# Other PSUM banks for two small pieces of a fused block: the first w1 group and the first segment's attention

## The chip, the cores and the metric

The kernel runs on one core of one Trainium2 chip. The time of a run is the device time in microseconds. Before the change six runs gave a median of 1535.79 us (1535.21 to 1541.54). One further execution was recorded by the hardware profiler; all rows shown here come from it, and their times are microseconds from the start of its span.

## What is computed

Cut to what matters (all inputs bf16):

```python
xn = layernorm(A_x)                                  # 2048 tokens of 1024
return A_x + _A_ref(xn, ...) + _B_ref(xn, ...)

def _A_ref(x, mem0, Wq, Wk, Wv, Wo, seg_len):        # 32 heads of 128, 8 memory rows, segments of 32
    mem = mem0
    for s in range(64):
        h = concat([mem, x[32 * s : 32 * s + 32]])   # 40 rows
        q, k, v = h @ Wq, h @ Wk, h @ Wv
        o = softmax(mask(q @ k.T * scale)) @ v @ Wo  # memory rows see all, tokens causally
        mem = o[:8]
        outs.append(o[8:])

def _B_ref(x, w1, w2, w3, w4):
    h = gelu(layernorm(x) @ w1)
    x1 = x + shifted(h) @ w2                         # four quarters of the columns, shifted by -1, +1, -2, +2 tokens
    return x1 + gelu(layernorm(x1) @ w3) @ w4
```

## The kernel before

TensorE (PE in the profile) does all products, into PSUM, which the kernel divides by hand: a ring of four banks, one bank a tile (`mm_tile`, lines 132 to 133), and two groups of two banks each, "A" and "B", one tile at a time in each (`aux_tile`, line 135). A new tile in "A" or "B" must wait until everything that reads the old one is done. Every engine works in the order in which the program issues its instructions: the order is written out by hand, and no scheduler changes it.

The work goes in four stages.

*Stage 1, the product with w1 (lines 170 to 313).* Tokens are in 16 tiles of 128 rows. For each tile VectorE (DVE) takes mean and variance (`ln_stats`, L202 to L206; the power on GpSimd, POOL, L207), and `ln_apply` (L218) writes the normalised rows. These are transposed to xn2T: for tiles 0 to 3 on PE (`pe_trans`, L247), with the first half of the columns copied out by DVE (L250) and the second by ScalarE (ACT, L252); from tile 4 on by a transposing DMA (`dma_trans`, L223). Two tiles make a group g of 256 tokens. For each group there are eight column tiles `co` of 128 outputs, each a chain of eight matmuls of 256 columns over the contraction (L262) and then a gelu on ACT (L264). Between column tiles 3 and 4 of a group, ACT normalises tiles of x in place (`normalise_x`, L235): four of them in group 1, two in later groups. After each group `seg_sums` (L257) forms two small products, in "A" and "B". `warm(n)` issues n matmuls of 512 columns on a constant (L197).

Group 0 is written apart (L270 to L296). Its first six column tiles do the first four contraction steps, as soon as half of w1 is there. They are held in the four ring banks and in group "A", one bank each. Then tiles 2 and 3 are normalised and transposed, both through group "B", then come the second halves, and then column tiles 6 and 7 whole.

*Stages 2 and 3* are the product with w2 and the second layernorm (L329 to L343), and the products with w3 and w4 (L502, L520). They are not touched, but at the end of stage 3 the buffers of the attention are set up (`att_prep`).

*The attention.* Blocks b of 512 tokens, eight steps hg in each, four heads in a step; a step makes Q (L567), K (L583) and V (L590) in twelve chains c = 0 to 11. Between chains stand hooks for the step before (p) and the one before that (pp): `scores(p, m)` for m = 0 to 3 at c = 0, 3, 6, 9, into "A" (L612), read by the exponentials on ACT (L616); and `values` into "B" (L642), read by an addition on DVE (L646) and then a small copy on ACT (L650). `values(pp, 3)` stands at c = 1, and `values(p, 0)`, `(p, 1)`, `(p, 2)` at c = 4, 7, 10. Between the exponentials and L646 stand, on DVE, the softmax of the scores (L618 to L631), whose result `BD` the values of that m use one or more chains later.

In block 0 the first segment has the given memory mem0, and so each of its eight steps also does a small ordinary attention over 40 rows, in the following step (i = 1 to 8), through three hooks:

- `first_soft` at c = 2: psVZ (L666, four products that turn the memory's values), copied out by ACT (L667), and psZ (L671, the scores), read by DVE (L673), then a softmax on DVE and ACT (L675 to L681)
- `first_trans` at c = 6: psZT (L687), copied out by ACT (L689)
- `first_values` at c = 8: psZO (L695), read by DVE (L696) and ACT (L697)

All four take a bank of the ring. Their operands have 8 or 40 rows or columns, so the weight loads have shapes 128x8, 128x40, 40x40 and 40x128. `first_scores` (L654 to L661) copies the operands together on POOL. In steps 5 to 7 DVE also prepares the next block's input, `make_xm` (L469), at c = 2, 6 and 10.

*The end.* `out_part` multiplies the attention's output with Wo, 32 matmuls of 512 columns for a tile (L740), DVE adds what the other branch left (L746) and a DMA stores the tile (L748). The last tile is `out_chain(b, 7)` (L900).

Of the kernel before, what the change touches and what calls it, by code (L numbers as in the profile page):

```python
# [21 lines left out]
P = 128  # L22
# [41 lines left out]
def kernel(  # L64
# [98 lines left out]
    with ExitStack() as keepx:  # L163
# [6 lines left out]
        with ExitStack() as p0:  # L170
# [65 lines left out]

            def pe_trans(n):
                xn2 = xn2s.pop(n)
                if n < 2:
                    ps = [mm_tile("psT")[:], mm_tile("psT")[:]]  # L240
                else:
                    t = aux_tile([P, 2, 512], "B", "psT")
                    ps = [t[:, 0, :], t[:, 1, :]]
                for h in range(2):
                    p3_ = ps[h].rearrange("p (k t) -> p k t", k=4)
                    for k in range(4):
                        nc.tensor.matmul(p3_[:, k, :], xn2[:, (4 * h + k) * P:(4 * h + k + 1) * P], ident[:], start=True, stop=True)  # L247
                    dst = xn2Ts[n // 2][:, n % 2, 4 * h:4 * h + 4, :]
                    if h == 0:
                        nc.vector.tensor_copy(dst, p3_)  # L250
                    else:
                        nc.scalar.copy(dst, p3_)  # L252
# [22 lines left out]
            warm(2)  # L275
            ln_apply(1)
            pe_trans(1)
            warm(2)
            normalise_x(0)
            normalise_x(1)  # L280
            first = [mm_tile("ps1")[:, 0:256] for _ in range(4)]
            t = aux_tile([P, 2, 512], "A", "ps1")
            first += [t[:, 0, 0:256], t[:, 1, 0:256]]
            for co in range(6):
                w1_part(0, co, first[co], range(4))
            ln_stats(2)
            ln_stats(3)
            for n in (2, 3):
                ln_apply(n)
            for n in (2, 3):  # L290
                pe_trans(n)
            for co in range(6):
                w1_part(0, co, first[co], range(4, KT))
            stage1(0, (6, 7))
            seg_sums(0)
            seg_sums(1)  # L296
            ln_stats(4)
# [54 lines left out]
    with ExitStack() as p3:  # L352
# [130 lines left out]
        def att_prep():  # L483
            load_xT(0)
            for nm in "qkv":
                need_w(nm, 0)
            need_w("q", 1)
            make_xm(0)
            sm = A["sm"]
            A["BD"] = [sm.tile([P, 4, TW], BF16, name=f"BD{i}") for i in range(3)]  # L490
            A["EQ"] = [sm.tile([P, 4, W], F32, name=f"EQ{i}") for i in range(2)]
            for t in A["EQ"]:
                nc.gpsimd.memset(t[:, :, SEG:W], float(M))
            A["SS"] = sm.tile([P, 4], F32, name="SSsum")
            nc.gpsimd.memset(A["SS"][:], 0.0)

# [43 lines left out]
    def hsl(hg):  # L540
        return slice(4 * hg, 4 * hg + 4)
# [96 lines left out]
    def values(s, m):  # L638
# [10 lines left out]
            VM[:, hsl(s.hg), z + j0:z + 4].unsqueeze(3).to_broadcast((P, 4, 4 - j0, SEG)), op=ALU.add)  # L649
        nc.scalar.copy(oTm[:, hsl(s.hg), z:z + 4], p4[:, :, :, SEG])  # L650

    def first_scores(s):
        QZ = smp.tile([P, 4, L], BF16, tag="QZ", name="QZ")
        KZ = smp.tile([P, 4, L], BF16, tag="KZ", name="KZ")  # L654
        nc.gpsimd.tensor_copy(QZ[:, :, 0:SEG], s.Q[:, :, 0:SEG])
        nc.gpsimd.tensor_copy(QZ[:, :, SEG:L], QM[:, hsl(s.hg), 0:M])
        nc.gpsimd.tensor_copy(KZ[:, :, 0:SEG], s.K[:, :, 0:SEG])
        nc.gpsimd.tensor_copy(KZ[:, :, SEG:L], s.K[:, :, 512:512 + M])
        s.VZ = smp.tile([L, 512], BF16, tag="VZ", name="VZ")
        nc.gpsimd.tensor_copy(s.VZ[0:SEG, :], s.V[0:SEG, 0, :])  # L660
        s.QZ, s.KZ = QZ, KZ  # L661

    def first_soft(s):
        pv = mm_tile("psVZ")
        for hh in range(4):
            nc.tensor.matmul(pv[SEG:L, hh * P:(hh + 1) * P], VM[:, 4 * s.hg + hh, 0:M], ident[:], start=True, stop=True)  # L666
        nc.scalar.copy(s.VZ[SEG:L, :], pv[SEG:L, :])  # L667
        ps = mm_tile("psZ")
        p3_ = ps[0:L, 0:4 * L].rearrange("p (h k) -> p h k", h=4)
        for hh in range(4):  # L670
            nc.tensor.matmul(p3_[:, hh, :], s.QZ[:, hh, :], s.KZ[:, hh, :], start=True, stop=True)  # L671
        e = smp.tile([L, 4, L], F32, tag="eZ", name="eZ")
        nc.vector.scalar_tensor_tensor(e[:], p3_, SCALE, mask40[0:L, :].unsqueeze(1).to_broadcast((L, 4, L)), op0=ALU.mult, op1=ALU.add)  # L673
        mx = smp.tile([L, 4], F32, tag="mxZ", name="mxZ")
        nc.vector.tensor_reduce(mx[:], e[:], axis=AX.X, op=ALU.max)  # L675
        nc.vector.tensor_tensor(e[:], e[:], mx[:].unsqueeze(2).to_broadcast((L, 4, L)), op=ALU.subtract)
        nc.scalar.activation(e[:], e[:], ACTF.Exp)
        nc.vector.tensor_reduce(mx[:], e[:], axis=AX.X, op=ALU.add)
        nc.vector.reciprocal(mx[:], mx[:])
        s.PZ = smp.tile([L, 4, L], BF16, tag="PZ", name="PZ")  # L680
        nc.vector.tensor_tensor(s.PZ[:], e[:], mx[:].unsqueeze(2).to_broadcast((L, 4, L)), op=ALU.mult)  # L681

    def first_trans(s):
        ps = mm_tile("psZT")
        p3_ = ps[0:L, 0:4 * L].rearrange("p (h k) -> p h k", h=4)
        for hh in range(4):
            nc.tensor.matmul(p3_[:, hh, :], s.PZ[:, hh, :], ident[0:L, 0:L], start=True, stop=True)  # L687
        s.PZT = smp.tile([L, 4, L], BF16, tag="PZT", name="PZT")
        nc.scalar.copy(s.PZT[:], p3_)  # L689

    def first_values(s):
        ps = mm_tile("psZO")
        p3_ = ps[:, 0:4 * L].rearrange("p (h k) -> p h k", h=4)
        for hh in range(4):
            nc.tensor.matmul(p3_[:, hh, :], s.VZ[:, hh * P:(hh + 1) * P], s.PZT[:, hh, :], start=True, stop=True)  # L695
        nc.vector.tensor_copy(oX[:, hsl(s.hg), 0:SEG], p3_[:, :, 0:SEG])  # L696
        nc.scalar.copy(oZ[:, hsl(s.hg), :], p3_[:, :, SEG:L])  # L697

    rms = {}

# [30 lines left out]

    parts = {}

    def out_part(b, c, h0, h1):
        m, ch = divmod(c, 2)
        if h0 == 0:
            parts[b, c] = mm_tile("psP")
        ps = parts[b, c]
        for h in range(h0, h1):
            nc.tensor.matmul(ps[:], oX[:, h, m * P:(m + 1) * P], wo_sb[:, h, ch * 512:(ch + 1) * 512], start=(h == 0), stop=(h == H - 1))  # L740
        if h1 < H:
            return
        cc = slice(ch * 512, (ch + 1) * 512)
        Rt = Rts.pop((b, c))
        ot = iop.tile([P, 512], BF16, tag="ot", bufs=2, name="ot")
        nc.vector.tensor_tensor(ot[:], ps[:], Rt[:], op=ALU.add)  # L746
        eng = nc.sync if b == NB - 1 else nc.gpsimd
        eng.dma_start(out_v[:, 4 * b + m, cc], ot[:])  # L748
        if c + 2 < 8:
            load_Rt(b, c + 2)  # L750

    def out_chain(b, c):
# [50 lines left out]
    for i in range(NS):  # L803
# [7 lines left out]
        def at(c, f, *a):  # L811
            hooks.setdefault(c, []).append((f, a))
# [10 lines left out]
                at(2 + 4 * (k % 3), make_xm, s.b + 1, (k,))  # L823
        if fz:
            at(2, first_soft, p)
            at(6, first_trans, p)
            at(8, first_values, p)
            first_scores(p)
        if s.hg == 1 and s.b > 0:
# [38 lines left out]
        if last:  # L868
            b = s.b
            load_Rt(b, 0)  # L870
            load_Rt(b, 1)
            hp = H - 4
            scores(s, 0)
            values(p, 3)
            out_part(b, 0, 0, hp)
            scores(s, 1)
            values(s, 0)
            out_part(b, 1, 0, hp)
            scores(s, 2)
            values(s, 1)  # L880
            out_part(b, 0, hp, H)
            out_part(b, 1, hp, H)
            out_part(b, 2, 0, hp)
            scores(s, 3)
            values(s, 2)
            out_part(b, 3, 0, hp)
            values(s, 3)
            out_part(b, 2, hp, H)
            out_part(b, 3, hp, H)
            norm_sums(b)  # L890
            for j in range(4):
                norm_recip(b, j)
            norm_apply(b)
            norm_add(b)
            out_chain(b, 4)
            out_chain(b, 5)
            verify()
            out_chain(b, 6)
            verdict()
            out_chain(b, 7)  # L900

    main.close()
    cond = nc.values_load(flag_i[0:1, 0:1], min_val=0, max_val=NV + 1)
# [126 lines left out]
```

## Time and profile before

| what | value |
|---|---|
| median of six runs | 1535.79 us |
| time of the profiled execution | 1534.74 us |
| its span | 1533.0 us |
| PE busy | 1506.6 us, 98% of the span |
| VectorE (DVE) busy | 662.5 us, 43% |
| ScalarE (ACT) busy | 450.4 us, 29% |
| GpSimd (POOL) busy | 232.0 us, 15% |
| granted PE clock over the span | 0.998 |
| one step of block 0 in the attention (psS of step 2 to psS of step 3) | 26.7 us |

How to read the rows: a row of the time-ordered view gives the start, the duration, the engine, the line of the kernel, the operation, what is written from what, the shape and how many instructions were merged; in brackets, for how long the engine was idle before it and which instruction's end released it. A merged row of several matmuls lasts until the last of them has ended, and the next one can start before that, since matmuls are pipelined. "PEld" rows are the weight loads ahead of the matmuls. The table by stretches gives for each stretch its length, the busy time of each engine with the number of instructions in parentheses, the granted PE clock (1.00 is full speed), the busy share of the DMA engines and GB/s.

### The profile page before, as it was taken

Reading aid. Unit: us, or ns where it says so; the run is one execution under the profiler, and the core shown is the slowest. Engines: PE = TensorE matmul, PEld = TensorE weight load, DVE = VectorE, ACT = ScalarE, POOL = GpSimd, SP = SyncE. Lnnn points to the kernel's source line nnn. Section 1 sums busy time; section 2 is a strip of 40 time slices with the busy share of each in tenths; the row PEclk is TensorE's granted clock in tenths of the full one; section 3 lists DMA queues with packets and bytes.
Section 4 is the critical chain, followed back from the end, with each engine's and each line's share of the span. In section 5 each row is a group of like instructions: output and inputs, shape, how many; then the busy total and the mean of one; then the engine's idle time right before and its main releaser. Section 6 shows DMA issues by size and latency. Waiting matters only on the chain.

```text
span 1533.0 us, 23861 instructions
## 1 busy us (share of the span) xinstructions
PE 1506.6 (98%) x9425; PEld 792.3 (52%) x9552; DVE 662.5 (43%) x1562; ACT 450.4 (29%) x1241; POOL 232.0 (15%) x640
## 2 busy tenths in 40 slices
PE   7999999999999999999999999999999999999998
PEld 5944444444444466666544544444544444444445
DVE  7275010010110225666632767731667641676652
ACT  4633202103012034444410443320443420334320
POOL 3133020111110111212110111110111110111100
PEclk9999999999999999999999999999999999999999
DMA  6679653454121545474422454431454441344211
GB/s 185 168 217 304 225 178 105 149 179 153 62 90 42 191 140 177 139 203 155 152 86 66 138 165 138 152 103 49 137 162 143 139 131 55 115 142 142 88 36 36
DMA packets 190885, 208.38 MB, mean 136 GB/s; under 512 B 51176, under 2 KB 158712, under 8 KB 190768
## 3 DMA queue, kind: packets, MB, share of 16 engines
q1 hardware_dynamic: 183520, 182.49, 39.6%
q0 software_dynamic: 7248, 24.31, 4.1%
q8 instruction: 77, 1.26, 0.4%
q14 instruction: 40, 0.33, 0.1%
HBM read 170.07 MB, written 25.17 MB: 127 GB/s over the span
## 4 chain that ended last, share of the span: by engine, by line
PE 92%; DVE 5%; ACT 1%; DMA 1%; issue 1%; SPq 0%; POOL 0%; ACTq 0%; DVEq 0%
PE psP L740 14%; PE psV L590 14%; PE psK L583 13%; PE ps L502 13%; PE ps L520 13%; PE psQ L567 12%; PE ps L329 4%; PE ps L262 3%; PE psO L642 2%; PE psS L612 2%; PE psM L599 1%; DMA x<-in_A_x_dram 1%; ACT ET L616 1%; DVE Q L574 1%; DVE BD L631 1%
## 5 line engine op out<-in xcount | busy, mean ns | idle before, releaser
L740 PE MATMUL psP<-wo_sb,oX 128*128 128x512 bf16 x1003 | 221.4, 379 | 1.1
L616 ACT ACTIVATE ET<-psS 32x132 f32<-32x132 f32 x512 | 139.0, 272 | 196.3 <-PE psS L612 191.1
L520 PE MATMUL ps<-w,hT_all 128*128 128x512 bf16 x874 | 193.7, 379 | 1.2
L583 PE MATMUL psK<-xT,w 128*128 128x512 bf16 x747 | 176.4, 379 | 1.1
L567 PE MATMUL psQ<-xT,w 128*128 128x512 bf16 x750 | 175.9, 379 | 1.5 <-DVE Q L574 0.4
L590 PE MATMUL psV<-w,xT 128*128 128x512 bf16 x745 | 175.1, 379 | 1.0
L583 PEld LDWEIGHTS <-w 128*128 128x128 bf16 x1280 | 121.4, 98 | 81.2 <-issue 0.8
L740 PEld LDWEIGHTS <-oX 128*128 128x128 bf16 x1024 | 99.7, 98 | 118.4
L567 PEld LDWEIGHTS <-w 128*128 128x128 bf16 x1024 | 97.0, 98 | 105.6 <-issue 2.9
L503 ACT ACTIVATE hT_all<-ps 128x512 bf16<-128x512 f32 x112 | 66.7, 597 | 283.9 <-PE ps L502 283.9
L520 PEld LDWEIGHTS <-hT_all 128*128 128x128 bf16 x896 | 87.0, 98 | 103.9
L650 ACT CAST oTm<-psO 128x16 bf16<-128x16 f32 x128 | 23.0, 179 | 355.9 <-DVE oX L646 355.9
L618 DVE STREAM_TRANSPOSE EQ<-ET 128x128 f32<-128x128 f32 x128 | 39.7, 310 | 184.0 <-ACT ET L616 184.0
L574 DVE TENSOR_TENSOR Q<-psQ,QM 128x512 bf16<-128x512 f32 (+1 forms) x128 | 85.6, 678 | 61.6 <-ACT Q L573 42.3
L633 POOL TENSOR_TENSOR BD<-ET,c_segone_sb 128x16 bf16<-128x16 f32 x128 | 33.9, 265 | 517.3 <-ACT ET L616 517.3
L590 PEld LDWEIGHTS <-xT 128*128 128x128 bf16 x768 | 72.1, 98 | 73.5
L502 PE MATMUL ps<-xn3T,w3a 128*128 128x512 bf16 x448 | 97.7, 379 | 0.0
L502 PE MATMUL ps<-xn3T,w3b 128*128 128x512 bf16 x448 | 97.7, 379 | 0.0
L631 DVE TENSOR_TENSOR BD<-PT,c_segone_sb 128x512 bf16<-128x512 bf16 x128 | 89.9, 702 | 4.4
L746 DVE TENSOR_TENSOR ot<-psP,Rt 128x512 bf16<-128x512 f32 x32 | 22.0, 691 | 156.2 <-PE psP L740 156.2
L646 DVE TENSOR_TENSOR oX<-psO,VM 128x512 bf16<-128x512 f32 (+1 forms) x128 | 86.3, 674 | 2.0 <-PE psO L642 2.0
L433 DVE TENSOR_SCALAR xt<-xt,lnst 128x1024 bf16<-128x1024 bf16 x16 | 8.7, 546 | 181.1 <-POOL R L432 181.1
(149 smaller groups left out, 1608.9 us busy)
## 6 DMA issues: line engine op xcount, KB each, us to landing
w<-in_A_Wq_dram SPq DMA_DIRECT2D x32, 1024.0 KB, 5.7
w<-in_A_Wk_dram SPq DMA_DIRECT2D x32, 1024.0 KB, 5.8
w<-in_A_Wv_dram SPq DMA_DIRECT2D x32, 1024.0 KB, 5.7
R_scratch<-x POOLq DMA_DIRECT2D x16, 512.0 KB, 6.0
R<-R_scratch SPq DMA_DIRECT2D x16, 512.0 KB, 7.7
chunk<-in_A_Wv_dram SPq DMA_DIRECT2D x8, 1024.0 KB, 6.4
R_scratch<-R POOLq DMA_DIRECT2D x16, 512.0 KB, 6.6
chunk<-in_A_Wo_dram SPq DMA_DIRECT2D x8, 1024.0 KB, 6.4
```

Source lines behind the costliest of these rows:

```text
L329: nc.tensor.matmul(ps[:], hTB[:, k, o:o + P], w2_sb[:, k, ch * 512:(ch + 1) * 512], start=(k == 0), stop=(k == KT - 1))
L502: nc.tensor.matmul(ps[:], w3[:, k, (f % FH) * P:(f % FH + 1) * P], xn3Ts[tb][:, :, k, :], start=(k == 0), stop=(k == KT - 1))
L503: nc.scalar.activation(h3T[:, f, :], ps[:], ACTF.Gelu_apprx_tanh)
L520: nc.tensor.matmul(ps[:], h3T[:, f, j * P:(j + 1) * P], w4t[f // 4][:, f % 4, ch * 512:(ch + 1) * 512], start=(f == 0), stop=(f == FT - 1))
L567: nc.tensor.matmul(ps[:], w[:, k, hh * P:(hh + 1) * P], s.xm[:, k, 0:512], start=(k == 0), stop=(k == KT - 1))
L574: nc.vector.tensor_tensor(q3[:, j0:16, 0:SEG], p3_[:, j0:16, :], QM[:, 4 * s.hg + hh, z + j0:z + 16].unsqueeze(2).to_broadcast((P, 16 - j0 ...
L583: nc.tensor.matmul(ps[:, 0:c], w[:, k, hh * P:(hh + 1) * P], s.xm[:, k, h2 * c:(h2 + 1) * c], start=(k == 0), stop=(k == KT - 1))
L590: nc.tensor.matmul(ps[:], s.xm[:, k, m * P:(m + 1) * P], w[:, k, :], start=(k == 0), stop=(k == KT - 1))
L616: nc.scalar.activation(ET[q, :, :], ps[q, :, W * j:W * (j + 1)], ACTF.Exp, scale=SCALE)
L631: nc.vector.tensor_tensor(B4[:, :, :, 0:SEG], PT[:].unsqueeze(2).to_broadcast((P, 4, 4, SEG)), so.unsqueeze(3).to_broadcast((P, 4, 4, SEG) ...
L646: nc.vector.tensor_tensor(oX[:, hsl(s.hg), m * P:(m + 1) * P].rearrange("p h (j i) -> p h j i", i=SEG)[:, :, j0:4, :], p4[:, :, j0:4, 0:SE ...
L740: nc.tensor.matmul(ps[:], oX[:, h, m * P:(m + 1) * P], wo_sb[:, h, ch * 512:(ch + 1) * 512], start=(h == 0), stop=(h == H - 1))
```

## The change

There are three edits.

1. **Group 0 of stage 1.** All eight column tiles do their first four contraction steps at once. They lie two to a bank in the four banks of "A" and "B"; only the first of a bank starts the accumulation with the start flag. The second halves follow in pairs, each pair with its two gelus, and the transposes of tiles 2 and 3, now always in ring banks, stand after the second and third pair. The `warm(2)` ahead of the group is gone.
2. **The small attention.** The operands QZ, PZ, VZ and a new one, VMZ, are 128 rows or columns wide, with zeros beyond the 40 or 8 that count; they are allocated once and cleared on POOL in `att_prep`. One more POOL copy a step fills VMZ. Their products go to "A" (psZ, psZT) and "B" (psVZ, psZO) instead of the ring. `first_trans` moves from c = 6 to c = 5.
3. **The last output tile** is done in two halves of 256 columns, each with its own addition and store.

```diff
 def pe_trans(n):
-    if n < 2:
-        ps = [mm_tile("psT")[:], mm_tile("psT")[:]]
-    else:
-        t = aux_tile([P, 2, 512], "B", "psT")
-        ps = [t[:, 0, :], t[:, 1, :]]
+    ps = [mm_tile("psT")[:], mm_tile("psT")[:]]
...
 pe_trans(1)
-warm(2)
 normalise_x(0)
 normalise_x(1)
-first = [mm_tile("ps1")[:, 0:256] for _ in range(4)]
-t = aux_tile([P, 2, 512], "A", "ps1")
-first += [t[:, 0, 0:256], t[:, 1, 0:256]]
-for co in range(6):
-    w1_part(0, co, first[co], range(4))
+first = []
+for tag in "AB":
+    t = aux_tile([P, 2, 512], tag, "ps1")
+    first += [t[:, c // 2, (c % 2) * 256:(c % 2 + 1) * 256] for c in range(4)]
+
+def w1_first(co, ks):
+    for k in ks:
+        nc.tensor.matmul(first[co], w1_sb[:, k, co * P:(co + 1) * P], xn2Ts[0][:, :, k, :],
+                         start=(k == 0 and co % 2 == 0), stop=(k == KT - 1), skip_group_check=True)
+
+def w1_first_out(c):
+    for co in c:
+        nc.scalar.activation(hTB[:, co, 2:258], first[co], ACTF.Gelu_apprx_tanh)
+
+for co in range(KT):
+    w1_first(co, range(4))
 ln_stats(2)
 ln_stats(3)
 for n in (2, 3):
     ln_apply(n)
-for n in (2, 3):
-    pe_trans(n)
-for co in range(6):
-    w1_part(0, co, first[co], range(4, KT))
-stage1(0, (6, 7))
+for c0 in range(0, KT, 2):
+    w1_first(c0, range(4, KT))
+    w1_first(c0 + 1, range(4, KT))
+    w1_first_out((c0, c0 + 1))
+    if c0 in (2, 4):
+        pe_trans(c0 // 2 + 1)
 seg_sums(0)
 seg_sums(1)
 ln_stats(4)
...
+for nm in ("QZ", "PZ", "VMZ"):
+    A[nm] = sm.tile([P, 4, P], BF16, name=nm)
+    nc.gpsimd.memset(A[nm][:], 0.0)
+A["VZ"] = sm.tile([P, 512], BF16, name="VZ")
+nc.gpsimd.memset(A["VZ"][:], 0.0)
...
 def first_scores(s):
+    nc.gpsimd.tensor_copy(VMZ[:, :, SEG:L], VM[:, hsl(s.hg), 0:M])
...
 def first_soft(s):
-    pv = mm_tile("psVZ")
+    pv = aux_tile([P, 512], "B", "psVZ")
     for hh in range(4):
-        nc.tensor.matmul(pv[SEG:L, hh * P:(hh + 1) * P], VM[:, 4 * s.hg + hh, 0:M], ident[:], start=True, stop=True)
-    nc.scalar.copy(s.VZ[SEG:L, :], pv[SEG:L, :])
-    ps = mm_tile("psZ")
+        nc.tensor.matmul(pv[:, hh * P:(hh + 1) * P], VMZ[:, hh, :], ident[:], start=True, stop=True)
+    nc.scalar.copy(VZ[SEG:2 * SEG, :], pv[SEG:2 * SEG, :])
+    ps = aux_tile([P, 4, L], "A", "psZ")
...
 def first_trans(s):
-    ps = mm_tile("psZT")
+    ps = aux_tile([P, 4, L], "A", "psZT")
...
 def first_values(s):
-    ps = mm_tile("psZO")
+    ps = aux_tile([P, 4, L], "B", "psZO")
...
-def out_part(b, c, h0, h1):
+def out_part(b, c, h0, h1, nsp=1):
...
     at(2, first_soft, p)
-    at(6, first_trans, p)
+    at(5, first_trans, p)
     at(8, first_values, p)
...
-out_chain(b, 7)
+out_part(b, 7, 0, H, 2)
```

More of the change, by code (lines that the diff above doesn't have):

```diff
@@ L277 @@
             pe_trans(1)
-            warm(2)
             normalise_x(0)
             normalise_x(1)
-            first = [mm_tile("ps1")[:, 0:256] for _ in range(4)]
-            t = aux_tile([P, 2, 512], "A", "ps1")
-            first += [t[:, 0, 0:256], t[:, 1, 0:256]]
-            for co in range(6):
-                w1_part(0, co, first[co], range(4))
+            first = []
[4 more added lines that the diff above has]
+                for k in ks:
+                    nc.tensor.matmul(first[co], w1_sb[:, k, co * P:(co + 1) * P], xn2Ts[0][:, :, k, :], start=(k == 0 and co % 2 == 0),
+                                     stop=(k == KT - 1), skip_group_check=True)
+            def w1_first_out(c):
[3 more added lines that the diff above has]
+                w1_first(co, range(4))
             ln_stats(2)
@@ L650, in values @@
         nc.scalar.copy(oTm[:, hsl(s.hg), z:z + 4], p4[:, :, :, SEG])
+    QZ, PZ, VMZ, VZ = A["QZ"], A["PZ"], A["VMZ"], A["VZ"]
     def first_scores(s):
-        QZ = smp.tile([P, 4, L], BF16, tag="QZ", name="QZ")
-        KZ = smp.tile([P, 4, L], BF16, tag="KZ", name="KZ")
+        s.KZ = smp.tile([P, 4, L], BF16, tag="KZ", name="KZ")
         nc.gpsimd.tensor_copy(QZ[:, :, 0:SEG], s.Q[:, :, 0:SEG])
         nc.gpsimd.tensor_copy(QZ[:, :, SEG:L], QM[:, hsl(s.hg), 0:M])
[L657 to L661, printed above, removed]
+        nc.gpsimd.tensor_copy(s.KZ[:, :, 0:SEG], s.K[:, :, 0:SEG])
+        nc.gpsimd.tensor_copy(s.KZ[:, :, SEG:L], s.K[:, :, 512:512 + M])
+        nc.gpsimd.tensor_copy(VMZ[:, :, SEG:L], VM[:, hsl(s.hg), 0:M])
+        nc.gpsimd.tensor_copy(VZ[0:SEG, :], s.V[0:SEG, 0, :])
     def first_soft(s):
-        pv = mm_tile("psVZ")
+        pv = aux_tile([P, 512], "B", "psVZ")
         for hh in range(4):
-            nc.tensor.matmul(pv[SEG:L, hh * P:(hh + 1) * P], VM[:, 4 * s.hg + hh, 0:M], ident[:], start=True, stop=True)
-        nc.scalar.copy(s.VZ[SEG:L, :], pv[SEG:L, :])
-        ps = mm_tile("psZ")
-        p3_ = ps[0:L, 0:4 * L].rearrange("p (h k) -> p h k", h=4)
+            nc.tensor.matmul(pv[:, hh * P:(hh + 1) * P], VMZ[:, hh, :], ident[:], start=True, stop=True)
+        nc.scalar.copy(VZ[SEG:2 * SEG, :], pv[SEG:2 * SEG, :])
+        ps = aux_tile([P, 4, L], "A", "psZ")
         for hh in range(4):
-            nc.tensor.matmul(p3_[:, hh, :], s.QZ[:, hh, :], s.KZ[:, hh, :], start=True, stop=True)
+            nc.tensor.matmul(ps[:, hh, :], QZ[:, hh, :], s.KZ[:, hh, :], start=True, stop=True)
         e = smp.tile([L, 4, L], F32, tag="eZ", name="eZ")
-        nc.vector.scalar_tensor_tensor(e[:], p3_, SCALE, mask40[0:L, :].unsqueeze(1).to_broadcast((L, 4, L)), op0=ALU.mult, op1=ALU.add)
+        nc.vector.scalar_tensor_tensor(e[:], ps[0:L, :, :], SCALE, mask40[0:L, :].unsqueeze(1).to_broadcast((L, 4, L)), op0=ALU.mult, op1=ALU.add)
         mx = smp.tile([L, 4], F32, tag="mxZ", name="mxZ")
@@ L679, in first_soft @@
         nc.vector.reciprocal(mx[:], mx[:])
-        s.PZ = smp.tile([L, 4, L], BF16, tag="PZ", name="PZ")
-        nc.vector.tensor_tensor(s.PZ[:], e[:], mx[:].unsqueeze(2).to_broadcast((L, 4, L)), op=ALU.mult)
+        nc.vector.tensor_tensor(PZ[0:L, :, 0:L], e[:], mx[:].unsqueeze(2).to_broadcast((L, 4, L)), op=ALU.mult)
     def first_trans(s):
-        ps = mm_tile("psZT")
-        p3_ = ps[0:L, 0:4 * L].rearrange("p (h k) -> p h k", h=4)
+        ps = aux_tile([P, 4, L], "A", "psZT")
         for hh in range(4):
-            nc.tensor.matmul(p3_[:, hh, :], s.PZ[:, hh, :], ident[0:L, 0:L], start=True, stop=True)
-        s.PZT = smp.tile([L, 4, L], BF16, tag="PZT", name="PZT")
-        nc.scalar.copy(s.PZT[:], p3_)
+            nc.tensor.matmul(ps[:, hh, :], PZ[:, hh, :], ident[:, 0:L], start=True, stop=True)
+        s.PZT = smp.tile([P, 4, L], BF16, tag="PZT", name="PZT")
+        nc.scalar.copy(s.PZT[:], ps[:])
     def first_values(s):
-        ps = mm_tile("psZO")
-        p3_ = ps[:, 0:4 * L].rearrange("p (h k) -> p h k", h=4)
+        ps = aux_tile([P, 4, L], "B", "psZO")
         for hh in range(4):
-            nc.tensor.matmul(p3_[:, hh, :], s.VZ[:, hh * P:(hh + 1) * P], s.PZT[:, hh, :], start=True, stop=True)
-        nc.vector.tensor_copy(oX[:, hsl(s.hg), 0:SEG], p3_[:, :, 0:SEG])
-        nc.scalar.copy(oZ[:, hsl(s.hg), :], p3_[:, :, SEG:L])
+            nc.tensor.matmul(ps[:, hh, :], VZ[:, hh * P:(hh + 1) * P], s.PZT[:, hh, :], start=True, stop=True)
+        nc.vector.tensor_copy(oX[:, hsl(s.hg), 0:SEG], ps[:, :, 0:SEG])
+        nc.scalar.copy(oZ[:, hsl(s.hg), :], ps[:, :, SEG:L])
     rms = {}
@@ L732 @@
     parts = {}
-    def out_part(b, c, h0, h1):
+    def out_part(b, c, h0, h1, nsp=1):
         m, ch = divmod(c, 2)
+        w = 512 // nsp
         if h0 == 0:
[L737 to L749, printed above, removed]
+            parts[b, c] = [mm_tile("psP") for _ in range(nsp)]
+        for q in range(nsp):
+            ps = parts[b, c][q]
+            cc = slice(ch * 512 + q * w, ch * 512 + (q + 1) * w)
+            for h in range(h0, h1):
+                nc.tensor.matmul(ps[:, 0:w], oX[:, h, m * P:(m + 1) * P], wo_sb[:, h, cc], start=(h == 0), stop=(h == H - 1))
+            if h1 < H:
+                continue
+            if q == 0:
+                Rt = Rts.pop((b, c))
+            ot = iop.tile([P, 512], BF16, tag="ot", bufs=2, name="ot")
+            nc.vector.tensor_tensor(ot[:, 0:w], ps[:, 0:w], Rt[:, q * w:(q + 1) * w], op=ALU.add)
+            eng = nc.sync if b == NB - 1 else nc.gpsimd
+            eng.dma_start(out_v[:, 4 * b + m, cc], ot[:, 0:w])
+        if h1 == H and c + 2 < 8:
             load_Rt(b, c + 2)
```

## The prediction

> **What bounds the kernel now.** I read the page's busy shares and chain first, then the time-ordered rows of the three places that the diff edits: the first 37 us, the attention steps of block 0 (540 to 770 us), the last 12 us.
>
> ```profile
> PE 1506.6 (98%) x9425; PEld 792.3 (52%) x9552; DVE 662.5 (43%) x1562; ACT 450.4 (29%) x1241; POOL 232.0 (15%) x640
> PE 92%; DVE 5%; ACT 1%; DMA 1%; issue 1%; SPq 0%; POOL 0%; ACTq 0%; DVEq 0%
> ```
>
> TensorE (PE) is the bound, and from about 36 us on it hardly rests. So whatever moves PE's stream in one of the three places moves the end one for one, unless a later wait takes it back.
>
> *The head.* Rows of PE and ACT, in order of time (start, duration, engine, line, count, idle time before):
>
> ```profile
> 10.73 2.78 PE L262 MATMUL ps<-xn2T,w_sb 128*128 128x256 bf16 x24
> 19.51 4.47 PE L262 MATMUL ps<-xn2T,w_sb 128*128 128x256 bf16 x20
> 24.45 2.56 PE L262 MATMUL ps<-xn2T,w_sb 128*128 128x256 bf16 x20 [0.47 <-ACT hT_all L264]
> 27.25 7.15 PE L262 MATMUL ps<-xn2T,w_sb 128*128 128x256 bf16 x64
> 31.22 4.62 ACT L235 ACTIVATE x<-x,nm,lnst 128x1024 bf16<-128x1024 bf16 x4
> 35.75 1.18 ACT L264 ACTIVATE hT_all<-ps 128x256 bf16<-128x256 f32 x4
> ```
>
> And the table by stretches (PE busy, then the other engines, granted PE clock, DMA):
>
> ```profile
> 11.25:14.66 3.41, 2.27 (x21) 1.77 (x19) 3.20 (x11) 1.82 (x2) 0.70 (x1) 1.00 0.95 355
> 14.66:18.08 3.42, 0.95 (x12) 0.72 (x13) 1.55 (x3) 0.59 (x1) 1.63 (x3) 1.00 0.09 32
> 18.08:21.50 3.42, 2.64 (x18) 1.88 (x16) 3.01 (x8) 1.01 (x3) 0.47 (x1) 0.50 0.02 5
> 21.50:24.92 3.42, 2.95 (x15) 1.88 (x14) 3.23 (x10) 1.50 (x4) 1.41 (x3) 0.50 0.09 17
> ```
>
> A matmul of 256 columns starts every 0.112 us at full clock (64 in 7.15), but every 0.22 us in the row at 19.51. After a stretch with PE busy only 0.95 of 3.42 us the clock is 0.50 for two such stretches. The poor stretch is the transposes of tiles 2 and 3, each half waiting for the one aux buffer to be copied out.
>
> *The small attention,* step 2 of block 0:
>
> ```profile
> 591.39 0.39 PE L612 MATMUL psS<-Q,K 128*128 128x132 bf16 x4
> 593.35 0.40 PE L642 MATMUL psO<-BD,V 128*128 128x132 bf16 x4
> 595.40 0.39 PE L666 MATMUL psVZ<-c_ident_sb,VM 128*8 128x128 bf16 x4
> 596.19 0.68 DVE L646 TENSOR_TENSOR oX<-psO,VM 128x512 bf16<-128x512 f32 x1
> 596.32 1.89 PE L567 MATMUL psQ<-xm,w 128*128 128x512 bf16 x8 [0.34 <-DVE Q L574]
> 596.90 0.18 ACT L650 CAST oTm<-psO 128x16 bf16<-128x16 f32 x1 [3.17 <-DVE oX L646]
> ...
> 606.21 0.40 PE L642 MATMUL psO<-BD,V 128*128 128x132 bf16 x4
> 608.27 0.27 PE L695 MATMUL psZO<-PZT,VZ 40*128 40x40 bf16 x4
> 608.52 0.68 DVE L646 TENSOR_TENSOR oX<-psO,VM 128x512 bf16<-128x512 f32 x1
> 609.24 0.18 ACT L650 CAST oTm<-psO 128x16 bf16<-128x16 f32 x1 [2.45 <-DVE oX L646]
> ```
>
> The thing to see: psO sits in bank group B until L650 ends, 3.7 us after its matmuls start (593.35 to 597.08) and 3.2 us in the lower pair (606.21 to 609.42), because L646 queues on DVE behind the softmax of the scores issued one chain earlier. The small attention's products go out 2.05 us after psO. Today that is harmless: they have banks of the mm ring. That PE truly waits for L650 before it refills B is seen once, in the last step:
>
> ```profile
> 1461.72 0.41 PE L642 MATMUL psO<-BD,V 128*128 128x132 bf16 x4 [1.04 <-ACT oTm L650]
> ```
>
> **Part 1, the first w1 group: -6.85 us.** Its first halves start at 10.73 as now, since the copy of xn2T that they need (DVE, 9.99 to 10.68) does not move. 32 x 0.112 = 3.6, to 14.3. The second half of w1 lands at 3.17 + 11.0 = 14.2 (DMA view): no wait. Tiles 0 to 3: 16 x 0.112 = 1.8, to 16.1. Transpose of tile 2 (DVE has its rows at 15.07): 8 in 0.5, to 16.6. Tiles 4, 5: 0.9, to 17.5. Transpose of tile 3 (rows at 16.2): to 18.0. Tiles 6, 7: to 18.9, outputs ready 19.2. The second seg_sums reuses B and must wait for the last two gelus, 2 x 0.39 on ACT, to about 20.0; then 0.3 of psX, and group 1 starts at 20.4 instead of 27.25. Of the 6.85 us, 40 matmuls in 4.5 instead of 7.5 us are some 3; the rest is transposes and gaps now filled.
>
> Does it reach the end? Group 2 starts today at 36.16, when the first gelu after four normalisations frees a bank (35.75 + 0.39); the chain view names a transposing DMA, but that one carries tile 8. ACT follows group 1 by itself: 20.4 + 8.9 = 29.3. Group 2 also needs the transpose of tile 5, issued at 25.63 today. DVE's copy for tile 3 moves from 18.38 to 17.85, so it goes out at 25.1; its neighbours land in 3.2 to 4.2, so 28.3 to 29.3, just in time. Group 4 needs tile 9 (36.06 + 6.9 - 0.5 = 42.5, wanted at 44.2), group 5 tile 11 (49.8, wanted at 51.6). All the gain stays; the least slack is about nothing at group 2, and a transpose 2 us late would take 2 us back. Clock: without the second warm(2) the stretch 7.83 to 11.25 has some 2.1 us of PE work instead of 2.62; 2.27 kept the clock, 0.95 lost it. Bounds: no loss, or two half-clock stretches (3.4 us). I take no loss, as 2.1 is near 2.27.
>
> **Part 2, the small attention: +17.6 us.** Padding changes the PE rows little: four 128-column products at the psT rate (0.056 each) 0.22, four 40-column ones between psX (16 in 0.54) and psM (64 in 2.39), so 0.13. That saves today's excess around the three visits. Step 2: the first visit takes 596.32 - 595.31 = 1.01 (psO at 593.35 + 0.23, then 8 x 0.216), of which 0.34 is a ring wait; psZT 0.38; psZO 0.29. Together 1.68, against 0.35 + 0.13 + 0.14 = 0.62: **-1.06 without waits.** Bounds for the padded rows: 0.5 to 1.0 a step.
>
> The Trainium skill ("TensorEngine Tiling (Array Packing)", Key Properties) says that changing the tiling mode drains TensorE. The weight loads of L666 and L695 here do show 0.42 us of issue idle ahead of them, but PE's stream loses only about 0.1 of it; by the page's rule alone the change would be a gain.
>
> Now the waits. (a) psVZ takes B after the previous step's last values. PE arrives at 595.31, L650 ends at 597.08: **1.8 us**. All of DVE's and ACT's work ahead of it is unchanged, and L650 ends 5.7 us after psS in each of steps 2 to 8. The q chain behind it starts at 597.13 + 0.35 = 597.5 instead of 596.32: **+1.2**. (b) psZ and psZT take A. The scores after them need L673 (597.77 + 0.31) and the copy L689. PE is late by then: the first is free, the second ends at about 605.1, when PE arrives. In step 1, which has no wait (a), these cost 1.0 and 0.8. (c) psZO takes B one chain after values 1. Later scores 1 go out at 599.22 (598.05 today), DVE's softmax follows at 600.8 (600.53; it was waiting on other DVE work), scores 2 at 605.14 (603.83). ACT exponentiates from 605.8 to 606.9 (2 K casts first), DVE's chain takes the 2.65 us of its rows, L646 0.68, L650 0.2: B is free at 610.35. PE arrives at 609.10: **1.3 us**. The v chain behind starts at 610.53 instead of 608.47: **+2.06 for step 2.** What queues behind both waits is all of PE: the next q or v chain. Nothing later in the step rests on PE, so nothing gives it back.
>
> The same walk for the others: step 1 +1.8; steps 2 to 4, 3 x 2.06 = 6.2; steps 5 to 7 put a 0.68 us make_xm on DVE ahead of L646, so wait (c) is 1.9 and wait (b) 0.35, less 0.55 that they lose today (psZT behind ACT 0.3, the ring 0.24): 2.06 + 0.6 + 0.35 - 0.55 = 2.4, three times 7.2; step 8, whose K casts are 0.59 for 512 columns, by the same walk +2.4. Sum 17.6. Ends: +8 if scores 2 and its softmax come 1.2 us earlier than I place them (wait (c) gone), +23 if wait (b) costs 0.7 in every step.
>
> The Trainium skill ("Perfetto Trace Analysis", Matmuls) wants independent groups rotated through different banks so that one's evacuation overlaps the next one's matmuls. This part gives up just that; the row at 1461.72 agrees with 1.04 us for one such reuse.
>
> Not on the path: one more POOL copy a step (like QZ's 0.22 us; POOL is 15% busy), four POOL memsets ahead of the attention, at most the 0.6 us of a 32x512 copy each, which would delay R1 sums due some 12 us later. If that cover were gone, 2 us.
>
> **Part 3, the last output tile in halves: -0.2 us.** 64 x 0.112 = 7.15 against 32 x 0.216 = 6.9: +0.25, less 0.1 for a shorter last matmul. The last add goes from 0.69 (512 wide) to 0.41 (the 252-wide row): -0.28. The last DMA carries half: 128 KB lands in 2.0, so 0 to -0.2. Bounds +0.1 to -0.3.
>
> **The sum.** The profiled execution took 1534.74 us (span 1533.0): 1534.74 - 6.85 + 17.6 - 0.2 = 1545.3. That execution is 1.05 below the median of the six runs, 1535.79; carried over, 1546.
>
> **Rivals.** *A: faster.* Bank group B comes free before PE arrives; only the saved PE time stays: 8 x -1.06 - 7.05 = -15.5, about 1520. It decides at wait (a) plus (c): below 7.05/8 + 1.06 = 1.9 us a step the change gains, above it loses; I find 3.1. For it: DVE is 43% busy overall. Against it: the L650 rows, alike in all eight steps. *B: one wait only,* (a) without (c): +8 - 7.05, about 1537, from 1533 to 1541. For it: (c) rests on a longer walk. *C: the head gives back 3 to 4 us* (transpose of tile 5, or the clock): 1549. For it: no slack at group 2. *D: wait (b) in every step:* 1552. *E: the change does not do what it says*, the tags not sharing banks: as A.
>
> **Chances.** Forecast with C, 1541 to 1550: 0.72. B: 0.12. D: 0.05. A with E: 0.11. The range takes in D and most of B: 1537 to 1552. A measurement of this kernel tells about 0.2% (3.1 us) from no change. Faster 0.11 (A, E), same 0.08 (the lower two thirds of B), slower 0.81.
>
> **What would show it.** Head right: clock 1.00 from 10 to 25 us, group 1 at about 20.4, group 2 at about 29.3. Attention right: idle time ahead of psVZ put down to oTm L650, 1.8 us in seven steps, ahead of psZO 1.2 to 2 in eight, and steps some 2 us longer than today's 26.7. Wrong: no such waits, or a head that is cold again.

## The result, and the profile after

The changed kernel takes 1543.22 us in the median of 34 runs (1542.93 to 1557.02), the kernel before, over all its runs by then, 1536.52 (71 runs, 1533.44 to 1553.48). The ratio is 1.0043, interval 1.0029 to 1.0057: slower by some 4 to 9 us. The prediction said 1546, between 1537 and 1552. The two profiled executions differ by 8.44 us (1534.74 and 1543.18), for which the prediction's sum had 10.6.

In the page after, PE does less and takes longer; its line, and the waits of PE in the order of their totals (who waited, for whom, us in total, times, longest):

```profile
PE 1499.3 (97%) x9456; PEld 793.0 (51%) x9582; DVE 663.9 (43%) x1563; ACT 453.3 (29%) x1241; POOL 234.6 (15%) x652
```

```profile
PE psVZ L678 <- ACT oTm L662: 11.6, 7, 1.7
PE psZO L703 <- ACT oTm L662: 10.4, 8, 1.7
...
PE ps L283 <- ACT hT_all L288: 1.0, 2, 0.7
...
PE psS L624 <- DVE eZ L684: 0.9, 1, 0.9
PE psX L253 <- ACT hT_all L288: 0.6, 1, 0.6
```

The two waits on top are 22 us that the kernel before did not have; lines are those of the changed kernel (its L662 is the copy that was L650). The head, in the time-ordered view of PE:

```profile
10.79 4.72 PE L283 MATMUL ps<-xn2T,w_sb 128*128 128x256 bf16 x40 [0.56 <-DVE xn2T L246]
16.26 1.03 PE L283 MATMUL ps<-xn2T,w_sb 128*128 128x256 bf16 x8 [0.75 <-ACT hT_all L288]
17.13 0.61 PE L243 MATMUL psT<-c_ident_sb,xn 128*128 128x128 bf16 x8
17.58 1.04 PE L283 MATMUL ps<-xn2T,w_sb 128*128 128x256 bf16 x8
18.45 0.61 PE L243 MATMUL psT<-c_ident_sb,xn 128*128 128x128 bf16 x8
19.36 1.03 PE L283 MATMUL ps<-xn2T,w_sb 128*128 128x256 bf16 x8 [0.30 <-ACT hT_all L288]
...
21.34 7.15 PE L258 MATMUL ps<-xn2T,w_sb 128*128 128x256 bf16 x64
...
30.26 7.15 PE L258 MATMUL ps<-xn2T,w_sb 128*128 128x256 bf16 x64 [1.39 <-ACT hT_all L260]
```

All of it runs at full clock, 0.11 us from one matmul to the next. Group 1 starts at 21.34 instead of 27.25, group 2 at 30.26 instead of 36.16: -5.9 us. Step 2 of the attention, the rows that answer to those of before:

```profile
586.76 0.39 PE L624 MATMUL psS<-Q,K 128*128 128x132 bf16 x4
...
588.72 0.40 PE L654 MATMUL psO<-BD,V 128*128 128x132 bf16 x4
...
588.96 1.89 PE L579 MATMUL psQ<-xm,w 128*128 128x512 bf16 x8
...
592.27 0.17 ACT L662 CAST oTm<-psO 128x16 bf16<-128x16 f32 x1 [3.17 <-DVE oX L658]
...
592.50 0.38 PE L678 MATMUL psVZ<-c_ident_sb,VMZ 128*128 128x128 bf16 x4 [1.65 <-ACT oTm L662]
...
602.43 0.40 PE L654 MATMUL psO<-BD,V 128*128 128x132 bf16 x4
...
602.67 1.89 PE L602 MATMUL psV<-w,xm 128*128 128x512 bf16 x7
...
605.37 0.18 ACT L662 CAST oTm<-psO 128x16 bf16<-128x16 f32 x1 [2.37 <-DVE oX L658]
...
605.61 0.25 PE L703 MATMUL psZO<-PZT,VZ 128*128 128x40 bf16 x4 [1.05 <-ACT oTm L662]
```

Both small products start right after the copy that frees B. The bracket counts idle time from the end of the last matmul, which lies some 0.16 us after the next one could have started: eight matmuls of 512 columns, one every 0.216 us from 588.96, would have let psVZ start at 590.69, so wait (a) is 1.8 us, and from 602.67 (one of the eight is not in the record) psZO could have started at 604.40, so wait (c) is 1.2. The lengths of the eight steps (first scores to first scores) in all kernels that follow:

| kernel | step 1 | 2 | 3 | 4 | 5 | 6 | 7 | 8 | sum |
|---|---|---|---|---|---|---|---|---|---|
| before | 26.73 | 26.68 | 26.68 | 26.67 | 27.29 | 27.28 | 26.17 | 24.23 | 211.7 |
| changed | 28.15 | 28.54 | 28.53 | 28.54 | 29.31 | 29.30 | 28.20 | 26.36 | 226.9 |
| no_a | 28.16 | 28.11 | 28.10 | 28.11 | 29.31 | 29.32 | 28.18 | 25.50 | 224.8 |
| no_c | 26.95 | 27.32 | 27.34 | 27.34 | 27.51 | 27.51 | 26.39 | 24.95 | 215.3 |
| no_ac | 26.95 | 26.90 | 26.90 | 26.91 | 27.51 | 27.51 | 26.40 | 24.24 | 213.3 |
| unpad_bank | 28.22 | 29.05 | 29.05 | 29.05 | 29.65 | 29.65 | 28.54 | 26.88 | 230.1 |
| att_pad_ring | 27.36 | 27.31 | 27.31 | 27.31 | 27.91 | 27.92 | 26.80 | 23.82 | 215.7 |
| ring_best | 26.52 | 26.48 | 26.48 | 26.48 | 27.08 | 27.08 | 25.97 | 23.82 | 209.9 |

So the account of the two profiled executions is: head -5.9, from there to the first scores -0.1, attention +15.2 (226.9 - 211.7), end -0.7, in all +8.5 against the measured 8.4.

One thing to know for what follows: single profiled executions also differ where nothing was edited. At the start of stage 3, PE waited 0 us in some executions and 3.8 to 11.1 in others; the step lengths above do not contain it, and I compare kernels by steps and starts, and by times only beside their intervals.

### The profile page after: what moved, and what is told of

It reads as the page before. It is cut to its first block, busy times and chain, and to the rows that moved or that the text cites. A ratio compares the mean times of both kernels' runs of the same rounds, so it can differ in the third digit from the quotient of the medians.

```text
span 1541.4 us, 23927 instructions
## 1 busy us (share of the span) xinstructions
PE 1499.3 (97%) x9456; PEld 793.0 (51%) x9582; DVE 663.9 (43%) x1563; ACT 453.3 (29%) x1241; POOL 234.6 (15%) x652
## 4 chain that ended last, share of the span: by engine, by line
PE 90%; DVE 6%; ACT 2%; issue 1%; DMA 0%; DVEq 0%; ACTq 0%
PE psP L751 14%; PE psV L602 13%; PE ps L514 13%; PE ps L532 12%; PE psK L595 12%; PE psQ L579 12%; PE ps L336 4%; PE ps L258 3%; PE psS L624 2%; PE psO L654 2%; ACT ET L628 1%; PE psM L611 1%; DVE BD L643 1%; DVE oX L658 1%; DVE Q L586 1%
## 5 line engine op out<-in xcount | busy, mean ns | idle before, releaser
L751 PE MATMUL psP<-wo_sb,oX 128*128 128x512 bf16 (+1 forms) x1036 | 221.5, 372 | 1.1
L751 PEld LDWEIGHTS <-oX 128*128 128x128 bf16 x1056 | 102.8, 98 | 115.5
L662 ACT CAST oTm<-psO 128x16 bf16<-128x16 f32 x128 | 22.9, 179 | 353.2 <-DVE oX L658 353.2
L596 ACT CAST K<-psK 128x512 bf16<-128x512 f32 (+1 forms) x160 | 79.6, 507 | 33.7 <-PE psK L595 33.1
L757 DVE TENSOR_TENSOR ot<-psP,Rt 128x512 bf16<-128x512 f32 (+1 forms) x33 | 22.2, 675 | 155.9 <-PE psP L751 155.9
```

The source lines that it names most:

```text
L596: nc.scalar.copy(s.K[:, hh, h2 * c:(h2 + 1) * c], ps[:, 0:c])
L751: nc.tensor.matmul(ps[:, 0:w], oX[:, h, m * P:(m + 1) * P], wo_sb[:, h, cc], start=(h == 0), stop=(h == H - 1))
```

## The experiments

My theory after the result: the whole loss is the sharing of A and B with the scores and values, through two waits on B, (a) ahead of psVZ and (c) ahead of psZO; padding is a small gain; the head's gain stays to the end and is partly the PE clock. The rivals: the padded rows cost PE time; PE's lateness is set by DVE's queue, however the waits are distributed; the head's gain is gaps alone.

**Each edit alone.** The kernel before with edit 1, with edit 2, and with edit 3, as in the diff of the change.

> The kernel before with edit 1 (group 0 of stage 1) alone. Theory (the three edits act in places that do not touch each other, and the head keeps its gain to the end): group 1 starts at about 21.3 us, group 2 at about 30.3, and the whole is 5.9 us shorter than before, about 1529 in the profiled execution. Rival (part of the head's gain is given back in stages 2 and 3, and the attention's loss is smaller than the step lengths say): less than 4 us shorter.

Group 1 at 21.06, group 2 at 29.97, steps like before's to 0.01 us, median 1529.24, ratio 0.9954 (0.9928 to 0.9981); the profiled execution 1529.18. The head's gain comes through whole.

> The kernel before with edit 2 (the small attention) alone. Theory: each of the eight steps is longer by what the changed kernel's steps are (1.4, three times 1.9, three times 2.0, 2.1), together +15.2 us, about 1550. Rival (the attention loses only because the earlier head shifts it against the weight transfers): less than +10 us.

Steps of 28.14, 28.52, 28.53, 28.54, 29.30, 29.30, 28.20 and 26.36: those of the changed kernel, +15.2 in all. Ratio 1.0109 (1.0054 to 1.0164). The attention's loss owes nothing to the head.

> The kernel before with edit 3 (last output tile in halves) alone. From the changed kernel's rows: the last addition ends 0.2 us earlier after the verdict's matmul, and what follows it is 3.3 instead of 3.9 us, so -0.8 us. As predicted: -0.2 us. Both are below what the times can tell; the profile's rows decide.

The ratio is 0.9995 (0.9963 to 1.0028), no answer, as expected. In the rows the last addition ends 0.2 earlier, counted from the small matmul of `verdict` that stands ahead of the last tile, and the span ends 3.3 us after it. Over all kernels here this last stretch is 3.9 to 4.8 us (mean 4.4 of 6) with one 128 KB store at the end and 3.3 to 3.4 (7 kernels) with 64 KB. So the edit is worth about 1.2 us, of which the pair of profiles above happened to show 0.7.

**Padding without sharing.** Edit 2 with this change, and head and end as before:

```diff
-pv = aux_tile([P, 512], "B", "psVZ")
+pv = mm_tile("psVZ")
-ps = aux_tile([P, 4, L], "A", "psZ")
+ps = mm_tile("psZ")[:, 0:4 * L].rearrange("p (h k) -> p h k", h=4)
```

(and the same for psZT and psZO).

> The kernel before with edit 2, but the four products stay in banks of the ring: padding without the sharing of A and B. Theory (bank waits are the whole loss, padding is a small gain): no wait of psVZ or psZO on the oTm copy, and 2 to 4 us shorter than before (psZT 0.25 and psZO 0.15 a step less, the ring wait of the q chain stays). Rival (operands padded to 128 rows cost PE time): longer than before by 5 us or more.

Neither came out: no wait on oTm is left in these steps, but they are 0.6 us longer than before, and the ratio is 1.0021 (0.9987 to 1.0055). PE's waits and the place in step 3, in the time-ordered view:

```profile
PE psK L588 <- ACT K L589: 8.0, 7, 1.3
...
PE psQ L572 <- DVE Q L579: 3.8, 7, 0.6
```

```profile
612.10 0.26 PE L689 MATMUL psZT<-c_ident_sb,PZ 128*128 128x40 bf16 x4
612.21 1.05 PE L588 MATMUL psK<-xm,w 128*128 128x260 bf16 x8
614.20 1.05 PE L588 MATMUL psK<-xm,w 128*128 128x260 bf16 x8 [0.95 <-ACT K L589]
```

psZT at c = 5 takes one bank of the ring between K chains, and the chain after next must wait for a K cast that ACT does late, since it is queued behind the oTm copy. The place, not the padding, costs the 0.95 of idle time: ring_best below has the same padding with first_trans back at c = 6, and its steps are 26.48, 0.83 shorter. So this run does not price padding.

**One wait at a time.** The changed kernel with psVZ alone (no_a), psZO alone (no_c), and both (no_ac) back in the ring; psZ and psZT stay in A.

> The changed kernel with psVZ back in a bank of the ring; psZ and psZT stay in A, psZO in B. Theory (the two waits on B are separate costs, both set by the oTm copy behind DVE's softmax): the 1.65 us ahead of psVZ go in seven steps; the wait ahead of psZO stays or grows to 1.5, since PE now comes earlier but the softmax does too, only in part. Steps 2 to 4 go from 28.5 to about 27.2 us, the whole about 9 us shorter than the changed kernel. Rival (PE is late by a fixed amount however it is distributed, because DVE's queue sets the step): psZO waits 2.7 us and the steps stay at 28.5.

Steps 2 to 4 at 28.1, only 0.43 shorter, steps 5 to 7 not at all (ratio to the kernel before 1.0055, 1.0030 to 1.0080): neither theory. The wait (c) keeps its 1.05, and two waits on A appear that step 2 of the changed kernel does not have: the scores after psZ wait 0.60 for DVE to read psZ (1.20 in steps 5 to 7), the scores after psZT wait 0.46 for ACT's copy. In the changed kernel, PE was too late to meet them.

> The changed kernel with psZO back in a bank of the ring; psVZ stays in B, psZ and psZT in A. Theory: the wait ahead of psZO goes (1.05 in steps 2 to 4, 1.65 in 5 to 7) and nothing replaces it, since the next tile in B (values 2) comes two chains later: steps 2 to 4 at 27.5, steps 5 to 7 at 27.65, the whole some 10 us shorter than the changed kernel. Rival: the wait moves to values 2, the steps stay at 28.5.

Steps of 27.3 and 27.5: 1.2 and 1.8 us shorter, as the theory had it; only (a), 1.66, is left. With psZO back in the ring, no new wait takes the place of (c). The ratio to the kernel before is 0.9974 (0.9948 to 1.0000).

> The changed kernel with psVZ and psZO in banks of the ring; psZ and psZT stay in A, first_trans at c = 5. Theory: both waits on B go, and with only psVZ and psZO in the ring the q chain behind them does not wait for a bank: steps 2 to 4 at 26.2 us (26.7 before), the whole about 18 us shorter than the changed kernel, near 1524 in the profiled execution. Rival (the padded rows cost PE time, or sharing A costs as much as sharing B): steps of 27 us or more.

No wait on B is left, but steps 2 to 4 are 26.90, not 26.2: 0.2 longer than before. The rows of step 2:

```profile
589.51 0.39 PE L678 MATMUL psVZ<-c_ident_sb,VMZ 128*128 128x128 bf16 x4
...
589.84 1.89 PE L579 MATMUL psQ<-xm,w 128*128 128x512 bf16 x8
592.33 0.39 PE L624 MATMUL psS<-Q,K 128*128 128x132 bf16 x4 [0.60 <-DVE eZ L684]
...
596.44 1.93 PE L595 MATMUL psK<-xm,w 128*128 128x260 bf16 x16
598.83 0.39 PE L624 MATMUL psS<-Q,K 128*128 128x132 bf16 x4 [0.46 <-ACT PZT L698]
```

These are 1.06 us of waits on A by the brackets, and 1.4 counted from when PE could have started (591.57 after the q chain, 598.2 after the K chains). Take them off and 25.5 is left, an estimate. So sharing A costs as well, once B does not hide it; the rival's second half was right in part (by the brackets 1.06 us on A here, 2.7 on B in the changed kernel). The median is 1529.89, ratio 0.9966 (0.9940 to 0.9991): with head and end of the change, faster than before.

**Sharing without padding.** The kernel before with only the banks of the four products changed, and first_trans at c = 5.

> The kernel before with only the banks of the small products changed: psVZ and psZO in B, psZ and psZT in A, first_trans at c = 5, operands of 8 and 40 rows as before; first group and end as before. Theory (padding is a gain of 0.3 to 0.5 us a step that the shared banks bury): steps 2 to 4 of 28.8 to 29.0 us, against 28.5 with padding. Rival (padding does nothing): 28.5. Rival (padding costs): less than 28.3.

29.05 in steps 2 to 4, 0.51 longer than with padding in the same banks. (a) and (c) are the same 1.66 and 1.05. So edit 2 is two things in these steps: sharing, with first_trans at c = 5, +2.37 us a step (29.05 - 26.68), and padding -0.51 (-0.34 in steps 5 to 7). The ratio is 1.0135 (1.0104 to 1.0167, two runs).

**The head's waits on gelus.**

```diff
-for c0 in range(0, KT, 2):
+for c0 in (0, 4, 2, 6):
...
-        pe_trans(c0 // 2 + 1)
+        pe_trans(2 if c0 == 4 else 3)
```

> The changed kernel with the second halves of the w1 column tiles in the pair order 0-1, 4-5, 2-3, 6-7 instead of 0-1, 2-3, 4-5, 6-7, the transposes after the second and third pair as before, so that two pairs running one after the other never lie in the same bank group. Theory (the waits of 0.75 and 0.30 us on a gelu come from the group being one tile: a pair waits for the gelus of the pair that shares its group, though not its bank): both waits go, group 1 starts at about 20.3 instead of 21.34. Rival (ACT is the limit of the head): the start of group 1 does not move by more than 0.3.

Both waits are gone; the time-ordered view:

```profile
10.76 5.40 PE L283 MATMUL ps<-xn2T,w_sb 128*128 128x256 bf16 x48 [0.56 <-DVE xn2T L246]
15.99 0.61 PE L243 MATMUL psT<-c_ident_sb,xn 128*128 128x128 bf16 x8
16.44 1.04 PE L283 MATMUL ps<-xn2T,w_sb 128*128 128x256 bf16 x8
...
17.76 1.04 PE L283 MATMUL ps<-xn2T,w_sb 128*128 128x256 bf16 x8
...
19.74 7.15 PE L258 MATMUL ps<-xn2T,w_sb 128*128 128x256 bf16 x64
```

Group 1 starts at 19.74, 1.6 earlier than in the changed kernel, more than the 1.05 of the two waits: counted from when PE could have started, as above, the two are 1.4; 0.2 stays unexplained. A pair had waited for the gelus of the pair in the same group, though they read another bank. That fits a wait kept for the group as one tile; no run gives the banks of a group tiles of their own. The times do not show the gain: the median is 1543.69 (1541.72 to 1555.20), and only the profiled execution, 1541.72, is 1.5 below that of the changed kernel.

**The clock of the head.** The kernel before, with matmuls on a constant in the places where PE waits between the transposes; their results go to columns that nothing reads.

```diff
+def busy(c):
+    for i in range(c):
+        nc.tensor.matmul(t[:, 0, 256:512], fill[:, 0:P], fill[:, 0:256], start=False, stop=False, skip_group_check=True)
+busy(13)
+pe_trans(2, busy, 10)
+busy(5)
+pe_trans(3, busy, 6)
```

(the second argument is called between the two halves of the transpose).

> The kernel before with 34 unused matmuls of 256 columns on a constant between the transposes of tiles 2 and 3, where PE waits, written to columns that nobody reads; nothing else is changed, so the order and the waits stay. Theory (about half of the head's 5.9 us is the PE clock lost in the stretch with PE nearly idle, the rest is gaps): the granted clock stays at 1.00 through 28 us, the 40 second-half matmuls take 4.5 to 4.9 instead of 7.5 us, group 1 starts at about 24.2 instead of 27.25. Rival (the gaps are all of the gain, the clock rows mislead): group 1 does not move.

The table by stretches (PE busy with instructions, the other engines, granted clock) and the first rows of group 0's second halves and group 1:

```profile
14.66:18.08 3.42, 3.06 (x32) 2.26 (x31) 1.37 (x3) 0.59 (x1) 1.49 (x3) 1.00 0.08 26
18.08:21.50 3.42, 3.25 (x31) 2.65 (x29) 3.25 (x8) 2.03 (x6) 0.70 (x1) 1.00 0.00 0
```

```profile
19.11 2.35 PE L264 MATMUL ps<-xn2T,w_sb 128*128 128x256 bf16 x20
21.93 2.34 PE L264 MATMUL ps<-xn2T,w_sb 128*128 128x256 bf16 x20 [0.47 <-ACT hT_all L266]
...
24.52 7.15 PE L264 MATMUL ps<-xn2T,w_sb 128*128 128x256 bf16 x64
```

With PE busy 3.06 us in the stretch where it had 0.95, the clock stays at 1.00, and group 1 comes 2.7 us earlier with no other change. But what the clock costs is not the same in every execution: with the head unchanged, group 1 starts at 27.25 in the profile before and in tail_only, at 26.74 in unpad_bank, 26.17 in att_pad_ring and 25.78 in att_only, and in the last two the clock is 0.50 for one stretch instead of two. So the clock is 1.3 to 2.7 us, and the pair compared here has the most of it. The 3.2 us from 24.52 to the changed kernel's 21.34, both at full clock, are gaps. Whether the whole kernel gains is not told by this run (ratio 1.0003, 0.9973 to 1.0033): its profiled execution lost 11.1 us at the start of stage 3.

**What the experiments point to.** The changed kernel with all four products in the ring, padded, first_trans back at c = 6, and the pairs in the order 0-1, 4-5, 2-3, 6-7.

> The changed kernel with all four small products back in banks of the ring (first_trans back at c = 6, operands padded) and the w1 pairs in the order 0-1, 4-5, 2-3, 6-7. Theory: no wait on A or B is left in the steps, padding saves what the mode changes cost, some 0.4 us a step, so steps 2 to 4 at 26.3 (26.7 before), group 1 at 19.7 (27.25 before), the end 0.8 shorter; together 1534.7 - 7.5 - 3.3 - 0.8, about 1523, faster than both. Rival (the ring is too small for the padded order too, as in the run with first_trans at c = 5): steps of 27.3, about 1531.

1524.73 us in the median, ratio 0.9926 (0.9911 to 0.9940): faster than both kernels. The gain is mostly the head's: group 1 starts at 19.73 instead of 27.25, and the eight steps are only 1.8 us shorter (209.9 against 211.7). Steps 2 to 4 are 26.48, 0.2 shorter than before; what padding saves is partly taken by the q chain, which still waits for a bank of the ring (0.54, 0.34 before):

```profile
587.78 0.39 PE L678 MATMUL psVZ<-c_ident_sb,VMZ 128*128 128x128 bf16 x4
588.01 0.26 PE L682 MATMUL psZ<-KZ,QZ 128*128 128x40 bf16 x4
588.80 1.89 PE L579 MATMUL psQ<-xm,w 128*128 128x512 bf16 x8 [0.54 <-DVE Q L586]
```

## Why the prediction was right, point by point

**The sum.** Forecast 1545.3 for the profiled execution, measured 1543.18; slower, as said, by the mechanism said. The two large terms were too large by 0.95 and by 2.4, in opposite directions; that these errors partly cancel is luck, and so is the base, since the head's gain depends on how long the clock of the kernel before was low (4.4 to 5.9 us, for group 1 at 25.78 to 27.25).

**The head, -6.85, measured -5.9.** Mis-sized by the two waits of 0.75 and 0.30: the prediction let pairs of column tiles follow each other freely inside one bank group, and counted the reuse of B only for seg_sums. The walk is otherwise right: the first halves at once, no wait for the second half of w1, the seg_sums wait (0.57), group 2 by ACT 8.9 us after group 1. The transpose of tile 5 went out at 26.13, not 25.1, since DVE's copy for tile 3 came at 18.88, not 17.85; group 2 did not wait for it. That the slack there is about nothing was right: in ring_best, group 2 does wait for this DMA and starts at 28.84, 0.2 later than in head_interleaved, which has the same head (28.66). The clock: the stretch 7.83 to 11.25 had 2.13 us of PE work (2.1 estimated) and kept 1.00.

**The attention, +17.6, measured +15.2.** Wait (a): psVZ starts 5.74 us after the first scores, as worked out (597.13 - 591.39); counted from when PE could have started the wait is 1.8, as said. Wait (c): psZO starts 18.85 us after them, 19.0 worked out; the wait is 1.2, and 1.3 was said. Step 2 came out at +1.86 instead of +2.06, since ACT's exponentials and so DVE's chain were 0.2 us earlier than placed. Steps 5 to 7: +2.02 instead of 2.4, wait (b) there 0.18 instead of 0.35. Step 1: +1.42 instead of 1.8 (wait (b) 0.95 and 0.40, where 1.0 and 0.8 stood). Step 8: +2.13 instead of 2.4.

**Padding, -1.06 a step "without waits".** The size was right, as the removal of padding cost and ring wait together: in no_ac the three visits take 0.33, 0.11 and 0.11 us of PE (589.51 to 589.84, 596.33 to 596.44, 602.79 to 602.90), 0.55 where 0.62 was worked out, and without its waits on A a step would be 1.2 below before (25.5, an estimate). Padding alone is 0.51 of it in shared banks, and 0.2 is left of it in the ring.

**The end, -0.2, measured -0.7 in this pair.** The addition was right (-0.2); the store was not: 64 KB instead of 128 ends the span 0.6 us sooner in this pair and 1.0 in the mean, beyond the bound of 0.3.

**The rivals.** A (faster, below 1.9 us of waits a step) did not come: 3.0 in steps 2 to 4 (2.7 by the brackets). Its account, that without the B waits only the saved PE time remains, is wrong: no_ac has neither wait and its steps are no shorter than before's, because A then makes PE wait. The prediction's "(b): the first is free" holds only behind wait (a). B, too, treated (a) and (c) as terms that add: taking (a) away saves 0.43, not 1.65, (c) 1.2. The kernel that B describes, (a) without (c), is no_c: its attention costs +3.6 (215.3 - 211.7), where B said +8. C did not come: the 0.95 that the head lost has another cause than the two named. D did not come, since behind wait (a) the scores of steps 2 to 4 find A free. E is refuted by the rows in which psVZ and psZO wait for oTm.

## What to carry to other kernels

- Before moving a product to other PSUM banks, walk the reuse: when the next tile wants the bank, and when the last reader of the present one ends, with everything queued ahead of that reader. Here the reader was a 0.18 us copy that ended 3.7 us after the matmuls had started, behind another product's softmax.
- Waits on shared banks are not a sum: one that is taken away can be replaced by the next (here 0.43 us of 1.65 were saved), so undo all sharing, or measure each removal.
- A bundle can hide a good edit in a bad one: by the rows the head, the padding and the half tile were all gains; the bank names of two products, psVZ and psZO, made the whole a loss (with these two back in the ring, no_ac, the ratio is 0.9966).

## What was not expected of the hardware

- A PE stretch of 3.4 us with little work was followed by one or two stretches at clock 0.50: 0.95 us of work in the kernel before, 0.82 in att_pad_ring, 0.86 in unpad_bank, 1.16 in att_only. With more work the clock stayed at 1.00: 1.43 us at the start of stage 3 in clock_fill, 1.87 in a step of the changed kernel, 2.13 in its head. So in these executions the limit lies between 1.16 and 1.43 us. The stretches are 3.41 us long and laid so that the clock changes at their ends. The two nearest to the limit, each with the one that follows it (att_only, then clock_fill):

```profile
14.70:18.12 3.42, 1.16 (x12) 0.81 (x13) 1.34 (x3) 0.58 (x1) 1.45 (x3) 1.00 0.02 7
18.12:21.53 3.41, 2.63 (x15) 1.97 (x15) 3.27 (x8) 1.28 (x3) 0.70 (x1) 0.50 0.02 5
...
140.98:144.39 3.41, 1.43 (x7) 0.56 (x6) 0.61 (x4) 1.04 (x1) 1.87 (x4) 1.00 1.26 107
144.39:147.80 3.41, 0.00 (x0) 0.00 (x0) 0.00 (x0) 1.69 (x3) 0.00 (x0) 1.00 1.14 322
```

- The stretch after the last addition was 3.9 to 4.8 us for a 128 KB store and 3.3 to 3.4 for 64 KB, over 13 kernels.
- The wait at the start of stage 3 (0 to 11.1 us, ahead of it ACT waiting for the transposing DMAs of stage 2) varied in kernels with the same code there. In the six executions with 3.8 us or more the clock was then 0.50 for 3.4 to 10.2 us, and the way from the first matmul of stage 3 to the first scores was 6.0 to 15.3 us longer than the 428.4 to 428.6 of the others. It is my reading that it makes much of the spread of the times (1533.4 to 1553.5 for one kernel); no run here tests what sets it.
